# Score bursts of up to six PSUM banks, and whole projection tiles between them, in a four-layer spectral and attention kernel

## The chip, the cores and the metric

The kernel runs on one core of one Trainium2 chip. The metric is the device time of one execution in microseconds (us). Each time shown is of a whole execution of the program on the device.

## What is computed

The input `x` has 2048 rows of 512. Four layers follow one another, each a residual on a layer norm: spectral mixing (A), segmented attention with a memory (B), A again and B again. All arithmetic is on 32-bit values.

```python
    def _A_ref(x, dft_seq_re, dft_seq_im, dft_hid_re, dft_hid_im):
        a = jnp.einsum("bsd,ed->bse", x, dft_hid_re)
        b = jnp.einsum("bsd,ed->bse", x, dft_hid_im)
        y = jnp.einsum("ts,bse->bte", dft_seq_re, a) - jnp.einsum("ts,bse->bte", dft_seq_im, b)
        return y
...
        for s in range(N):
            qs, ks, vs = q[:, :, s], k[:, :, s], v[:, :, s]
            logits = jnp.einsum("bhqd,bhkd->bhqk", qs, ks) * scale + mask
            p = _softmax(logits, axis=-1)
            a_dot = jnp.einsum("bhqk,bhkd->bhqd", p, vs)
            pq = phi(qs)
            num = jnp.einsum("bhld,bhde->bhle", pq, M)
            den = jnp.einsum("bhld,bhd->bhl", pq, z)[..., None] + 1e-6
            a_mem = num / den
            o = g * a_mem + (1.0 - g) * a_dot
            outs.append(o)
            pk = phi(ks)
            M = M + jnp.einsum("bhld,bhle->bhde", pk, vs)
            z = z + jnp.einsum("bhld->bhd", pk)
        o = (lambda x, *d: x.transpose(*d))(jnp.stack(outs, 2).reshape(B, H, S, Dh), 0, 2, 1, 3).reshape(B, S, D)
        return o @ wo

    x = A_x
    x = x + _A_ref(_layernorm(x, axis=-1), A_dft_seq_re, A_dft_seq_im, A_dft_hid_re, A_dft_hid_im)
    x = x + _B_ref(_layernorm(x, axis=-1), B_wq, B_wk, B_wv, B_wo, B_beta)
```

In B there are 32 heads of 16 columns, and 4 segments of 512 rows. Within a segment the softmax attention is causal; what earlier segments left is read through the memory `M` and `z`.

## The kernel before, in words

**Units, groups, segments.** An attention layer works segment by segment. A segment's 32 heads are four groups of eight heads, and a group is two units of four heads. A unit's four heads lie as two pairs: two ranges of partitions (`SIDES`, from rows 0 and 64) hold two heads each, so that one head of each side is multiplied at the same time on half of TensorE's rows each. There are 32 units in a layer and two attention layers.

**What is done for a unit.** `stack` (line 788) loads the queries and keys of the four heads from DRAM into the two row ranges. `natural_max` (line 811) computes the scores with queries on the partitions, in five steps; each step writes two PSUM banks, which VectorE reads with `tensor_tensor_reduce` (line 835) to take each row's maximum. The steps are, for each of the two heads of a side, query tile 3 alone and then tiles 0 and 2 together, and at last tile 1 of both heads. A sixth step turns the maxima into a high and a low part (`mparts`, lines 852 and 853). `max_rows` (line 859) transposes them on TensorE, copies them out on ScalarE (line 868) and writes them by DMA as two more rows beneath the stacked queries (line 871). `softmax_values` (line 877) then computes the scores transposed, with keys on the partitions and the maximum already subtracted, again in five steps of two banks. ScalarE takes a ReLU of the diagonal blocks (line 903) and the exponential of the bank (line 904); GpSimd zeroes what lies above the diagonal (`causal`, line 907). A last step, `pv`, multiplies the probabilities with the values: 16 products of 32 output columns, which fill one bank (`pv_bank`), copied out by ScalarE (line 969). `output` (line 978) transposes that back, scales it and adds it into `o_nat`.

**The other TensorE work.** `proj` (line 732) makes the queries or the keys of a group in one bank from twelve matmuls (four slices of the 512 columns, three products each, since a 32-bit value is split into a high and a low part). `values` (line 711) and `outproj` (line 1090) do the same for a tile of 128 rows. Besides these there are transposes (`prep`, `transpose_out`) and the memory's reads and updates (`mem_read`, `mem_update`). All these use the full array of 128 rows; the scores use 50 or 48 rows of each half, the `pv` products 32 columns each.

**PSUM.** Every TensorE result goes to a tile of one tag, `bank` (line 114), with eight buffers. A tile is free again when its last reader is done.

**The order of the work** is written out by hand. Every function above is a generator; `place` (line 186) puts its next step into a numbered slot with an order number inside the slot, and at the end all slots are run in order (lines 1287 to 1290). TensorE's instructions keep exactly this order (`keep_in_program_order`); the order on the other engines comes from the scheduler at build time, with a raised priority for the maxima (`URGENT`).

A unit has ten slots (`SU`), a group 20 (`SG`), a segment 80 (`SS`). Unit n starts at `t = t0 + 10 n`. Its softmax steps are in slots t, t+2, t+4, t+6 and t+8, its `pv` in t+12. The natural steps are in t-18 to t-10, two slots apart, so that softmax steps of one unit and natural steps of the next but one fall into the same even slots: five bursts of four banks in each unit, ten in a group. `max_rows` is in t-5 and `stack` in t-22. Projections, values and output tiles put three matmuls into a slot, over four slots (line 1215 and the lines above it). `light` (line 1162) names the slots of a unit that may take them, and `among` (line 1165) spreads eight steps over a stretch.

Of the kernel before, what the change touches and what calls it, by code (L numbers as in the profile page):

```python
# [10 lines left out]
F32 = mybir.dt.float32  # L11
# [7 lines left out]
P = 128  # L19
S, D, H = 2048, 512, 32  # L20
DH = D // H
NSEG = 4
# [36 lines left out]
def spectral_infini_kernel(  # L59
# [621 lines left out]
    def place_attention(x_in, x_out, t0, w_at, out_at):  # L681
# [195 lines left out]
        def softmax_values(s, g, u):  # L877
            qs, ks = stacks.pop((s, g, u, "q")), stacks.pop((s, g, u, "k"))
            K = KROWS + MROWS
            h0 = g * HG + u * HU  # L880

            def scores(dst, *cols):
                banks = [bank("sT") for _ in SIDES]
                off, diag = 0, []
                for p, kt in cols:
                    n = 512 - kt * P
                    for a, at in enumerate(SIDES):
                        T.matmul(
                            banks[a][:, off : off + n],
                            ks[at : at + K, p, kt * P : (kt + 1) * P],  # L890
                            qs[at : at + K, p, kt * P :],
                            start=True,
                            stop=True,
                        )
                    diag.append(off // P)
                    off += n
                for a, ps in enumerate(banks):
                    blocks = ps.rearrange("p (b c) -> p b c", c=P)
                    blocks = blocks[:, diag[0] : diag[-1] + 1 : max(1, diag[-1] - diag[0])]
                    if x_out is out_tiles and (s * NG + g) * NU + u >= NSEG * USEG - 3 and a:  # L900
                        V.tensor_scalar_max(blocks, blocks, 0.0)
                    else:
                        A.activation(blocks, blocks, AF.Relu)  # L903
                    A.activation(dst[a], ps, AF.Exp, scale=-SCALE)  # L904

            def causal(blocks):
                G.affine_select(  # L907
                    blocks,
                    blocks,
                    pattern=[[0, n] for n in blocks.shape[1:-1]] + [[1, P]],  # L910
                    compare_op=ALU.is_ge,
                    fill=0.0,
                    base=0,
                    channel_multiplier=-1,
                )
# [12 lines left out]

            p0, p1 = [], []
            events = {}  # L930

            def ev(t, f):
                events.setdefault(t, []).append(f)

            for p in range(HP):

                def first(p=p):
                    t = pair("pT", "wd", 8, F32)
                    p0.append(t)
                    scores((t[:, 0], t[:, 1]), (p, 0))  # L940
                    causal(t[:, :, :P])

                def second(p=p):
                    t = pair("pT", "wd", 8, F32)
                    p1.append(t)
                    scores((t[:, 0], t[:, 1]), (p, 1), (p, 3))
                    for c in 0, 3 * P:
                        causal(t[:, :, c : c + P])

                ev(6 + 2 * p, first)  # L950
                ev(2 + 2 * p, second)
            p2 = []

            def third():
                t = sb.tile([P, HU, 256], F32, name="pT2", tag="craw", bufs=2)
                p2.append(t.rearrange("p (a b) s -> p a b s", b=HP))
                scores([t[:, a * HP : (a + 1) * HP].rearrange("p h s -> p (h s)") for a in range(2)], (0, 2), (1, 2))
                causal(t[:, :, :P])

            ev(0, third)  # L960

            def last():
                pb = bank("pv_bank")
                pv(pb, 0, p0, 0)
                pv(pb, 1, p1, 0)
                pv(pb, 3, p1, 384)
                pv(pb, 2, [p2[0][:, :, p] for p in range(HP)], 0)
                ot = sb.tile([P, 512], F32, name="ot", tag="ut", bufs=8)
                A.activation(ot, pb, AF.Copy)
                outs[s, g, u] = ot  # L970

            ev(12, last)
            for t in range(13):
                for f in events.get(t, ()):
                    f()
                yield

        def output(s, g, u):
            ot = outs.pop((s, g, u))
# [179 lines left out]
        def unit(n):  # L1159
            return n // USEG, n % USEG // NU, n % NU  # L1160

        def light(t, n=SU):
            return [k for k in range(t, t + n) if (k - t0) % SU not in (2, 4)]

        def among(start, stop, n):
            at = light(start, stop - start)
            return [at[k * len(at) // n] for k in range(n)]

        def post(t):
            return [t + 1, t + 2, t + 3]  # L1170

# [2 lines left out]
            src = rows((wq, wk, wv, wo)[k // DT], d)  # L1174
            place(3, load_split(ws, (n, d), src, f"w{n}", "w", 16), [w_at(k) - 3, w_at(k)])
        for n in range(NSEG * USEG):
            t = t0 + SU * n
            place(0, softmax_values(*unit(n)), run_from(t, 13))
            place(1.9, output(*unit(n)), [t + 14])
            place(1.9, max_rows(*unit(n)), [t - (6 if x_out is out_tiles and n == NSEG * USEG - 1 else 5)])  # L1180
            place(1, natural_max(*unit(n)), run_from(t - 18, 5, 2), [t - 9])
            place(0.5, stack(*unit(n)), [t - 22])
        for s in range(NSEG):
            b = t0 + SS * s
            for j in range(2):
# [19 lines left out]
            for g in range(NG):  # L1205
# [126 lines left out]
```

## Time and profile before

| | |
|---|---|
| median of 3 runs | 1788.8 us (1785.93 to 1789.73) |
| the profiled execution | 1787.75 us, of which its span 1786.0 us |
| TensorE busy | 1745.4 us (98%), 10192 matmuls |
| VectorE busy | 1383.1 us (77%) |
| ScalarE busy | 1071.3 us (60%) |
| GpSimd busy | 357.7 us (20%) |
| mean granted TensorE clock | 0.993 |

The span is what the profiler records from the first instruction to the last; the execution's own time is a little longer. Names in the profile: `sT` is a bank of `softmax_values`, `nat` one of `natural_max`, `pT` the probabilities, `pqk` a projection, `pvv` a value tile, `po` an output tile, `on` and `oT` transposes of the outputs, `mT` the transpose of the maxima, `pM`, `pm` and `pkT` the memory's work, `m`, `u` and `y` the spectral layer. All matmuls have line 84, since a helper records them. PE is TensorE's matmuls, DVE VectorE, ACT ScalarE, POOL GpSimd, SPq the queue of the engine that issues most DMAs. A row of the timeline gives the start, the time to the end of the last one merged in it, and the count. Matmuls overlap in the records, so what TensorE spends on a row is read from its start to the start of the next.

### The profile page before, as it was taken

What the parts mean: (1) busy time and instruction counts of PE and PEld (TensorE: products, weight loads), DVE (VectorE), ACT (ScalarE), POOL (GpSimd) and SP (SyncE); (2) the same over time, 40 slices, a digit from 0 to 9 for tenths busy, and PEclk for the clock granted to TensorE, in tenths of its full rate; (3) what the DMA queues carried; (4) which work ended last, traced back from release to release, by engine and by line L of the source; (5) the groups of instructions that cost most, each with busy time, mean ns of one, the idle gap of its engine ahead of it and who ended that gap; (6) DMA issues with size and microseconds to landing.
All of it is one profiled execution on the core that took longest, in us unless ns stands there. A gap on an engine that the chain in (4) does not pass through costs nothing. (4 is left out here: it accounts for less than half of the span.)

```text
span 1786.0 us, 32579 instructions
## 1 busy us (share of the span) xinstructions
PE 1745.4 (98%) x10192; PEld 1266.5 (71%) x10192; DVE 1383.1 (77%) x4114; ACT 1071.3 (60%) x2388; POOL 357.7 (20%) x673
## 2 busy tenths in 40 slices
PE   8999999999999999999999999999999999999998
PEld 6888777887656666666578888888875666666655
DVE  8888978864777888877977997667658778787775
ACT  3344443432688777777764665444328787877775
POOL 1000000002232334344410000000123333333332
PEclk9999999999999999999999999999999999999999
DMA  8787775355455454555666877645546555555351
GB/s 284 244 263 254 232 249 167 106 177 159 143 153 139 142 147 111 157 129 130 170 207 215 264 236 232 195 147 149 176 130 183 134 131 151 132 132 155 91 131 44
DMA packets 145499, 303.10 MB, mean 170 GB/s; under 512 B 18096, under 2 KB 22192, under 8 KB 145328
## 3 DMA queue, kind: packets, MB, share of 16 engines
q1 hardware_dynamic: 138416, 288.44, 54.7%
q10 hardware_dynamic: 6912, 12.59, 1.8%
q8 instruction: 82, 1.34, 0.3%
q14 instruction: 89, 0.73, 0.1%
HBM read 211.83 MB, written 88.08 MB: 168 GB/s over the span
## 5 line engine op out<-in xcount | busy, mean ns | idle before, releaser
L835 DVE CUSTOM_DVE_ANT_0 junk<-nat,mask 128x512 bf16<-128x512 f32 (+3 forms) x1024 | 497.2, 486 | 178.9 <-PE nat L84 133.4
L904 ACT ACTIVATE pT<-sT 128x512 f32<-128x512 f32 x640 | 351.3, 612 | 0.7
L84 PE MATMUL m<-chi,xa 128*128 128x512 f32 x1056 | 308.6, 392 | 2.5 <-DVE c L524 2.1
L907 POOL TENSOR_SCALAR_AFFINE_SELECT pT<-pT 128x256 f32<-128x256 f32 (+1 forms) x448 | 193.3, 445 | 566.5 <-ACT pT L904 434.0
L84 PE MATMUL m<-clo,xa 128*128 128x512 f32 x720 | 230.8, 392 | 5.5 <-DVE clo L100 5.5
L84 PEld LDWEIGHTS m<-chi,xa 128*128 128x128 f32 x1056 | 198.1, 189 | 46.6 <-DVE c L524 2.9
L903 ACT ACTIVATE sT<-sT 128x256 f32<-128x256 f32 x625 | 179.7, 331 | 64.4 <-PE sT L84 63.5
L84 PE MATMUL y<-wdt,us 128*128 128x512 f32 x768 | 182.5, 391 | 0.2 <-DVE wdt L100 0.2
L84 PE MATMUL nat<-stkk,stkq 48*128 48x512 f32 (+3 forms) x1024 | 159.2, 345 | 8.4 <-DMA stkk<-scrk 5.6
L84 PE MATMUL sT<-stkq,stkk 50*128 50x256 f32 (+3 forms) x1024 | 164.8, 373 | 1.0 <-DMA stkq<-mt 0.8
L84 PEld LDWEIGHTS y<-wdt,us 128*128 128x128 f32 x768 | 143.4, 188 | 30.7 <-DVE wdt L100 0.9
L84 PEld LDWEIGHTS sT<-stkq,stkk 50*128 50x128 f32 x1024 | 84.4, 186 | 113.4 <-issue 53.0
L84 PEld LDWEIGHTS m<-clo,xa 128*128 128x128 f32 x720 | 135.2, 188 | 37.8 <-DVE clo L100 10.0
L84 PE MATMUL pv_bank<-pT,v_all 128*32 128x512 f32 (+3 forms) x2048 | 152.2, 437 | 1.7 <-DVE mx L835 1.7
L98 ACT ACTIVATE chi<-cring 128x512 fp32r<-128x512 f32 (+1 forms) x138 | 99.6, 727 | 86.0 <-PE m L84 35.8
L84 PEld LDWEIGHTS pv_bank<-pT,v_all 128*32 128x32 f32 x2048 | 59.2, 110 | 84.1 <-issue 82.8
L84 PE MATMUL pqk<-xT,wq 128*128 128x512 f32 x384 | 116.9, 425 | 0.0
L84 PEld LDWEIGHTS nat<-stkk,stkq 48*128 48x128 f32 x1024 | 96.5, 189 | 27.2 <-ACT pT L904 7.7
L84 PE MATMUL po<-wo,oh 128*128 128x512 f32 x384 | 114.5, 419 | 0.7 <-ACT oh L98 0.5
L147 POOL TENSOR_TENSOR r<-ve,half_neg 128x2 f32<-128x2 f32 (+2 forms) x24 | 19.9, 830 | 472.9 <-DVE ve L145 469.5
L84 PE MATMUL pvv<-wv,xT 128*128 128x512 f32 x384 | 114.1, 417 | 0.0
L84 PE MATMUL pqk<-xT,wk 128*128 128x512 f32 x384 | 108.5, 410 | 2.0 <-DVE mx L835 2.0
(187 smaller groups left out, 2830.4 us busy)
## 6 DMA issues: line engine op xcount, KB each, us to landing
cring<-in_ct SPq DMA_DIRECT2D x97, 256.0 KB
scrk<-parts SPq DMA_DIRECT2D x96, 256.0 KB
stkq<-scrq SPq DMA_DIRECT2D x128, 192.0 KB
stkk<-scrk SPq DMA_DIRECT2D x128, 192.0 KB
cring<-sum SPq DMA_DIRECT2D x95, 256.0 KB
xt<-mid SPq DMA_DIRECT2D x64, 256.0 KB
scrq<-parts SPq DMA_DIRECT2D x32, 512.0 KB
cring<-in_ct SPq DMA_DIRECT2D x27, 512.0 KB
```

Source lines behind the costliest of these rows:

```text
L84: return tc.keep_in_program_order(op(*args, **kwargs))
L98: pin(A.activation(hi, src, AF.Copy, scale=scale))
L147: G.tensor_tensor(out=r, in0=ve, in1=half_neg[:, :n], op=ALU.pow)
L835: last_max[0] = V.tensor_tensor_reduce(junk[:, :n], src, mask[:, 512 - n :], 1.0, 3e38, ALU.add, ALU.min, dst,)
L903: A.activation(blocks, blocks, AF.Relu)
L904: A.activation(dst[a], ps, AF.Exp, scale=-SCALE)
L907: G.affine_select(blocks, blocks, pattern=[[0, n] for n in blocks.shape[1:-1]] + [[1, P]], compare_op=ALU.is_ge, fill=0.0, base=0, channel ...
```

## The change

Two things are placed differently; no computation changes. Slots below are counted from `c`, the start of a group.

- **Scores.** The two units of a group get lists of their own. The first has its softmax steps in slots 0, 0, 3, 6 and 6 and its `pv` just before slot 12; the second in 9, 12, 12, 15 and 15 and just before slot 20. The natural steps, for the group that follows, are in 3, 3, 6, 9 and 9 (first unit) and 12, 15, 18, 18 and 20 (second unit). So the score steps fall into the slots 0, 3, 6, 9, 12, 15 and 18: seven bursts, six of three steps (six banks) and the last of two. The softmax steps take the order that they had: tile 2 of both heads, tiles 1 and 3 of each head, tile 0 of each head.
- **Tiles of twelve.** A projection, value or output tile puts its twelve matmuls into one slot: queries in slot 13 and keys in slot 16 for most groups, values at slots 4 and 7, output tiles at slots 1 and 7. The first two projections of a layer stay as they were, as do the output tiles of the last segment.

`max_rows` moves to 6 slots before the first unit's first softmax step (5 for the second), and `stack` to 7 slots before the first natural step (5 for the second unit).

```diff
-            p0, p1 = [], []
-            events = {}
...
-                ev(6 + 2 * p, first)
-                ev(2 + 2 * p, second)
...
+            def step(*cols):
+                t = pair("pT", "wd", 8, F32)
+                scores((t[:, 0], t[:, 1]), *cols)
+                for c in range(0, 512, 384)[: len(cols)]:
+                    causal(t[:, :, c : c + P])
+                return t
+
+            t = sb.tile([P, HU, 256], F32, name="pT2", tag="craw", bufs=2)
+            scores([t[:, a * HP : (a + 1) * HP].rearrange("p h s -> p (h s)") for a in range(2)], (0, 2), (1, 2))
+            causal(t[:, :, :P])
+            p2 = t.rearrange("p (a b) s -> p a b s", b=HP)
+            yield
+            p1, p0 = [], []
             for p in range(HP):
...
+                p1.append(step((p, 1), (p, 3)))
                 yield
+            for p in range(HP):
+                p0.append(step((p, 0)))
+                yield
+            pb = bank("pv_bank")
...
-            t = t0 + SU * n
-            place(0, softmax_values(*unit(n)), run_from(t, 13))
-            place(1.9, output(*unit(n)), [t + 14])
-            place(1.9, max_rows(*unit(n)), [t - (6 if x_out is out_tiles and n == NSEG * USEG - 1 else 5)])
-            place(1, natural_max(*unit(n)), run_from(t - 18, 5, 2), [t - 9])
-            place(0.5, stack(*unit(n)), [t - 22])
+            c = t0 + SG * (n // NU)
+            if n % NU == 0:
+                at, nat, pv_at, load, turn = (0, 0, 3, 6, 6), (3, 3, 6, 9, 9, 10), 12, -24, -6
+            else:
+                at, nat, pv_at, load, turn = (9, 12, 12, 15, 15), (12, 15, 18, 18, 20, 21), 20, -13, 4
+            if n == 0:
+                load = -22
+            place(0, softmax_values(*unit(n)), [c + k for k in at], [c + pv_at - 0.1])
+            place(1.9, output(*unit(n)), [c + pv_at + 2])
+            place(1.9, max_rows(*unit(n)), [c + turn])
+            place(1, natural_max(*unit(n)), [c - SG + k for k in nat])
+            place(0.5, stack(*unit(n)), [c + load])
...
-            place(2, values(s), *([light(b - 20), light(b)] if s else [run_from(b - 18, 8), light(b - 10)]))
+            place(2, values(s), *([k] * DT for k in ((b - 36, b - 16, b + 4, b + 7) if s else (b - 17, b - 13, b - 7, b - 2))))
...
-                free = light(o + 20) + light(o + 40) if s < NSEG - 2 else run_from(o + 20, DT * LT, 3)
+                free = [o + k for k in ((21, 27, 41, 47) if s < NSEG - 2 else (21, 27, 47, 67)) for _ in range(DT)]
...
-                    (0, 2): among(b, b + 13, 8),
-                    (0, 3): among(b + 13, b + 29, 8),
-                    (1, 0): among(b - 40, b - 29, 8),
-                    (1, 1): among(b - 29, b - 17, 8),
-                }.get((s, g), light(t - 50))
+                    (0, 2): [b + 1] * 4 + [b + 10] * 4,
+                    (1, 0): [b - 38] * 4 + [b - 33] * 4,
+                }.get((s, g), [t - 47] * 4 + [t - 44] * 4)
```

More of the change, by code (lines that the diff above doesn't have):

```diff
@@ L927, in pv @@
                     )
-            p0, p1 = [], []
-            events = {}
-            def ev(t, f):
-                events.setdefault(t, []).append(f)
-            for p in range(HP):
[L937 to L948, printed above, removed]
-                ev(6 + 2 * p, first)
-                ev(2 + 2 * p, second)
@@ L952, in softmax_values @@
[L952 to L975, printed above, removed]
-                yield
+            def step(*cols):
[6 more added lines that the diff above has]
+            scores([t[:, a * HP : (a + 1) * HP].rearrange("p h s -> p (h s)") for a in range(2)], (0, 2), (1, 2))
@@ new lines, in softmax_values @@
+            causal(t[:, :, :P])
+            p2 = t.rearrange("p (a b) s -> p a b s", b=HP)
+            yield
+            p1, p0 = [], []
+            for p in range(HP):
+                p1.append(step((p, 1), (p, 3)))
+                yield
+            for p in range(HP):
+                p0.append(step((p, 0)))
+                yield
+            pb = bank("pv_bank")
+            pv(pb, 0, p0, 0)
+            pv(pb, 1, p1, 0)
+            pv(pb, 3, p1, 384)
+            pv(pb, 2, [p2[:, :, p] for p in range(HP)], 0)
@@ L978, in output @@
+            ot = sb.tile([P, 512], F32, name="ot", tag="ut", bufs=8)
+            A.activation(ot, pb, AF.Copy)
+            outs[s, g, u] = ot
+            yield
         def output(s, g, u):
@@ L1160, in unit @@
             return n // USEG, n % USEG // NU, n % NU
[L1162 to L1167, printed above, removed]
         def post(t):
```

## The prediction

> **What bounds the kernel now.** I read the page first, for the engines' shares.
>
> ```profile
> span 1786.0 us, 32579 instructions
> PE 1745.4 (98%) x10192; PEld 1266.5 (71%) x10192; DVE 1383.1 (77%) x4114; ACT 1071.3 (60%) x2388; POOL 357.7 (20%) x673
> ```
>
> TensorE is busy nearly throughout, but its ends are modelled, so the share cannot say whether it runs at its peak. The windows view compares a stretch of the spectral layer with one segment (eight units) of attention.
>
> ```profile
> 1150.00:1200.00 50.00, 50.00 (x223) 41.40 (x222) 30.87 (x48) 23.40 (x37) 0.00 (x0) 1.00 0.55 171
> 580.40:697.10 116.70, 116.60 (x857) 76.50 (x856) 95.05 (x380) 90.17 (x224) 42.27 (x81) 1.00 0.52 137
> ```
>
> The columns are PE, PEld, DVE, ACT and POOL busy time. In the spectral stretch a 512-column matmul costs 50/223 = 0.224 us; the change leaves that layer alone. In attention a group (two units) takes 116.7/4 = 29.2 us, in which VectorE is busy 23.8 us and ScalarE 22.5 us. TensorE is the bound, and the other two are close behind. What TensorE does in that time shows in the timeline, by its start times.
>
> ```profile
> 661.71 0.50 PE L84 MATMUL sT<-stkq,stkk 50*128 50x512 f32 x2
> 662.05 0.40 PE L84 MATMUL nat<-stkk,stkq 48*128 48x512 f32 x2
> 662.38 1.66 PE L84 MATMUL pvv<-wv,xT 128*128 128x512 f32 x6
> 663.97 0.50 PE L84 MATMUL sT<-stkq,stkk 50*128 50x512 f32 x2
> ...
> 668.35 1.65 PE L84 MATMUL pqk<-xT,wq 128*128 128x512 f32 x6
> 669.93 2.36 PE L84 MATMUL pv_bank<-pT,v_all 128*32 128x512 f32 x32
> ...
> 672.22 0.50 PE L84 MATMUL sT<-stkq,stkk 50*128 50x384 f32 x4
> ```
>
> From 661.71 to 663.97 is 2.26 us. The two score steps each run two matmuls side by side on half the rows (50 or 48 of 128). If such a pair costs what one full 512-column matmul does, the stretch is 8 x 0.224 = 1.79 us of streaming. The other 0.47 us is the price of leaving the full array for the half-row form and coming back, so 0.235 us a change of form. The six matmuls from 668.35 to 669.93 take 1.58 us against 1.34, again 0.24 us over. TensorE's loss in attention is thus changes of form, not idle time.
>
> Two places of the same trace show what limits longer bursts: the eight banks of PSUM.
>
> ```profile
> 842.74 0.50 PE L84 MATMUL sT<-stkq,stkk 50*128 50x384 f32 x4
> 843.08 0.44 PE L84 MATMUL nat<-stkk,stkq 48*128 48x512 f32 x1
> 844.43 0.47 PE L84 MATMUL nat<-stkk,stkq 48*128 48x512 f32 x1 [0.91 <-DVE mparts L852]
> ```
>
> ```profile
> 1723.96 0.51 PE L84 MATMUL sT<-stkq,stkk 50*128 50x512 f32 x2
> ...
> 1724.30 0.41 PE L84 MATMUL nat<-stkk,stkq 48*128 48x512 f32 x2
> ...
> 1724.53 0.42 PE L84 MATMUL sT<-stkq,stkk 50*128 50x512 f32 x2
> ...
> 1725.49 0.56 PE L84 MATMUL nat<-stkk,stkq 48*128 48x128 f32 x4 [0.55 <-ACT pT L904]
> ```
>
> At 842.74 a four-bank burst stands right behind a value stage with little else near it: its last bank is still being read by VectorE, and TensorE waits 0.91 us. At 1723.96 eight banks are asked for in a row. The last step waits until ScalarE has finished the exponentials of the first, 1.53 us after that began.
>
> **The change, part by part: fewer changes of form.** By the slot lists, a group has had ten score bursts and two value stages, each stage directly ahead of a burst: 10 entries, 10 exits, 2 extra at the value stages, 22 changes. Afterwards there are seven bursts. Five are followed by full-array work (10 changes). The bursts of slots 9 and 18 go straight into a value stage and from it into the burst of slots 12 and 20 (4 changes). That is 14, 8 fewer. I take 0.225 us for one, a little under the measured 0.235 because those around the value stage are not separately seen: 8 x 0.225 = 1.8 us a group, and 32 groups (16 in each attention layer) make **58 us** off. If a sixth of them lie under a bank wait that is there anyway, it is 48 us.
>
> **Bank waits that come in.** What six banks take to drain follows from these rows of ScalarE, VectorE and GpSimd.
>
> ```profile
> 657.96 0.65 ACT L903 ACTIVATE sT<-sT 128x256 f32<-128x256 f32 x2
> 658.52 1.09 ACT L904 ACTIVATE pT<-sT 128x512 f32<-128x512 f32 x2
> ...
> 662.31 0.44 ACT L903 ACTIVATE sT<-sT 128x128 f32<-128x128 f32 x2
> 662.68 1.09 ACT L904 ACTIVATE pT<-sT 128x512 f32<-128x512 f32 x2
> ...
> 672.36 0.60 ACT L969 ACTIVATE ot<-pv_bank 128x512 f32<-128x512 f32 x1 [2.44 <-PE pv_bank L84]
> ```
>
> ```profile
> 658.15 0.69 DVE L835 CUSTOM_DVE_ANT_0 junk<-nat,mask 128x512 bf16<-128x512 f32 x1 [0.74 <-PE nat L84]
> ...
> 659.61 0.08 DVE L835 DVE_READ_ACCUMULATOR2_ANT mx<- 128x1 f32 x1
> ...
> 668.46 0.42 DVE L835 CUSTOM_DVE_ANT_0 junk<-nat,mask 128x256 bf16<-128x256 f32 x1 [0.17 <-PE nat L84]
> ...
> 670.32 0.09 DVE L835 DVE_READ_ACCUMULATOR2_ANT mx<- 128x1 f32 x1
> ...
> 675.45 0.28 DVE L835 CUSTOM_DVE_ANT_0 junk<-nat,mask 128x128 bf16<-128x128 f32 x1
> ...
> 677.19 0.08 DVE L835 DVE_READ_ACCUMULATOR2_ANT mx<- 128x1 f32 x1
> ```
>
> ```profile
> 659.67 0.77 POOL L907 TENSOR_SCALAR_AFFINE_SELECT pT<-pT 128x256 f32<-128x256 f32 x2 [2.80 <-ACT pT L904]
> ```
>
> First to last, a softmax step of two blocks holds ScalarE 1.65 us, one of key tile 0 1.46 us. A natural step of tile 3 (A) holds VectorE 1.54 us, the mixed one (B, 675.45 to 677.27) 1.82 us, the last (C, 668.46 to 670.41) 1.95 us. TensorE writes a step in 0.34 us, a further one of the same burst in 0.23 (1724.30 to 1724.53), so a burst of six banks in about 0.9 us. By bursts:
> - Slots 12 and 20, behind a value stage. The burst of slot 9 leaves VectorE B and C, 3.8 us; that of slot 18 A and B, 3.4 us. The value stage passes 2.29 us (669.93 to 672.22) and its own bank is held 0.74 us more (to 672.96). So the next burst, 3.2 us after the last one began, finds two or three of the eight banks taken and asks for six. The like of it is the 0.91 us row; the last bank is wanted only 0.6 us into the burst, so I take 0.5 us each, **1.0 us** a group.
> - Slot 3. In half the groups no output tile stands at slot 1, so only four transposes separate the bursts of slots 0 and 3 (0.49 us, next rows). The second starts about 1.65 us after the first, when one bank is untouched and one has come back (at 1.5 us). Its last step gets its banks at about 3.1 us, against 2.2, and the maxima of C, read by the transpose in slot 4, are ready at 3.5. I take 1.3 us there, **0.65 us** over all groups.
> - The value stage of the first unit needs the softmax steps of slot 6: 0.5 + 2 x 1.46 + 0.4 us of GpSimd, 3.8 us after the burst. TensorE gets there later where a tile of twelve stands between (12 x 0.224 = 2.7 us), about 0.9 us earlier where none does: **0.3 us** over all.
> - The bursts of slots 6, 9, 15 and 18 overlap the former one's drain by little: 0.1 us each, **0.4 us**.
>
> ```profile
> 675.07 0.66 PE L84 MATMUL on<-ident,ot 128*128 128x128 f32 x4
> 675.56 0.27 PE L84 MATMUL mT<-ident,mparts 128*72 128x128 f32 x1
> ```
>
> That is 2.35 us a group. Some of it replaces waits of today (the 0.91 us row is one); I credit 0.15 us. 32 x 2.2 = **70 us** on.
>
> **Edits that I cost at nothing.** The twelve matmuls in one go hold their bank 2.7 us in place of four or five slots; this is what lets six banks go to a burst, and it is in the sum. Stack loads and maxima rows move relative to their users:
>
> ```profile
> L868 ACT ACTIVATE mt<-mT 32x128 fp32r<-32x128 f32 x64 | 16.5, 258 | 7.2 <-PE mT L84 7.2
> ```
>
> ```profile
> 1738.15 5.37 DMA stkk<-scrk
> ...
> 1757.36 0.62 SPq L871
> ...
> 1758.03 1.92 DMA stkq<-mt
> ```
>
> A slot is 29.2/20 = 1.46 us. A load has had 4 slots (5.8 us) to its first use and gets 7 and 5 (10 and 7 us), so 5.4 us stays covered, the SP queue's own issues included. It must still wait for the buffer's last reader, now one slot ahead of it. The maxima have had 5 slots to the softmax and get 6 and 5, for 0.3 + 0.6 + 1.9 us. Uncovered, either costs about 1 us a group; a lead gained is worth nothing, since neither is waited for in most groups now. The last group of layer two has the same score work and no projections either way: 0, give or take 3 us.
>
> The sum is against the profiled execution's 1787.75 us (1786.0 of span and 1.75 around it; the median of the runs shown is 1.05 above): 1787.75 - 58 + 70 = **1800 us**.
>
> [...]
>
> **The rivals.**
> - *The changes of form decide* (faster). ScalarE and VectorE have 5 to 7 us free in each group of 29.2. If drains start earlier than I reckon, only the bursts behind the value stage wait, 0.9 us a group: 1787.75 - 58 + 29 = 1759 us; with no new wait at all, 1730. For it: at 1723.96 even eight banks in a row cost only 0.55 us. Against it: that burst found nothing else in PSUM.
> - *They cancel*: net waits of 1.7 to 1.9 us a group, 1785 to 1791 us.
> - *The maxima come late* (slower still). The row transpose of the second unit, slot 4, needs C of slot 0, and behind it hang the maxima's DMA and the softmax of slot 9. Where slots 1 to 3 are empty and VectorE is behind by over 1 us, this adds 1 us a group, 32 us: 1832 us.
> - *The clock falls.* Windows with waits have shown less than full clock:
>
> ```profile
> 500.00:550.00 50.00, 48.24 (x329) 30.75 (x328) 37.50 (x155) 41.36 (x104) 16.36 (x31) 0.93 0.52 140
> ```
>
> Here 7% of 50 us is lost, 3.5 us. If half the groups lost as much, it would be 56 us: 1856 us. Against it: steady segments with short waits run at 1.00. [...]
> - *The change does not do what it says*: TensorE's order is pinned, so the slot lists are what runs; no chance of its own.
>
> **How the numbers follow.** My forecast, waits above savings, 0.46; changes of form decide, 0.35; cancel, 0.09; late maxima, 0.07; clock, 0.03. So slower 0.56, same 0.09 (0.2% is 3.6 us, about what a measurement of this kernel can tell from no change), faster 0.35. The forecast's own part goes from 1792 to 1830 (waits of 3.1 us a group with no credit: 99 us on, 58 off). The rival on the fast side enters the range down to its 1759; what it has below, about 0.1, and the slow ones above 1832, about 0.08, stay out.
>
> **What would show it.** Right: in TensorE's timeline 14 changes of form a group, twelve projection matmuls in about 2.9 us, and waits of 0.3 to 1.3 us inside bursts released by ACT pT or DVE mx, most behind the value stage and at slot 3; VectorE's and ScalarE's busy totals as before. Wrong: steady groups under 28.5 us with bursts of six written in under 1.2 us; or the long waits standing at the row transpose or at a DMA; or a change of form that costs well under 0.2 us.

## The result, and the profile after

The changed kernel takes 1866.38 us (median of 4 runs, 1864.14 to 1872.38), the kernel before 1787.37 us in the runs beside it (1781.36 to 1789.73). The ratio is 1.045, with a 95% interval from 1.0415 to 1.049: slower by 79 us. The forecast was 1800 us, slower, with a range from 1759 to 1832 us.

The page of the changed kernel's profiled execution (1864.14 us), from the top:

```profile
span 1862.3 us, 32611 instructions
PE 1783.6 (96%) x10192; PEld 1334.9 (72%) x10192; DVE 1397.6 (75%) x4114; ACT 1067.3 (57%) x2388; POOL 358.4 (19%) x673
...
PEclk9999999999799999999899999999998999999998
```

VectorE, ScalarE and GpSimd do what they did before, to about 1%. The row of the granted clock was nothing but nines before; now it has a seven and three eights. The mean granted clock fell from 0.993 to 0.966. The traces record it as 1.00 or 0.50 and as nothing between (23 stretches at 0.50 in this span, 6 before), so twice what is missing to 1 is the share of time at half clock: 2 x 0.034 x 1862.3 = 127 us, against 25 us before.

The windows of the changed kernel show the spectral stretch, and the segment that the prediction took its 116.70 us from:

```profile
1150.00:1200.00 50.00, 50.00 (x222) 41.42 (x221) 30.85 (x48) 23.40 (x37) 0.00 (x0) 1.00 0.63 195
596.10:721.90 125.80, 120.87 (x858) 85.75 (x856) 96.45 (x382) 89.99 (x225) 42.27 (x81) 0.96 0.46 127
```

The spectral stretch is as it was. The segment, eight units with the same work, takes 9.1 us more, 2.3 us a group; at a clock of 0.96, 4% of 125.8 us or 5.0 us of that is clock.

TensorE's timeline of the changed kernel, in a stretch of that segment in which nothing goes wrong, and then where it does:

```profile
596.13 2.36 PE L84 MATMUL pv_bank<-pT,v_all 128*32 128x512 f32 x32
598.42 0.79 PE L84 MATMUL sT<-stkq,stkk 50*128 50x384 f32 x8
599.05 0.69 PE L84 MATMUL nat<-stkk,stkq 48*128 48x512 f32 x2
599.67 0.73 PE L84 MATMUL pm<-state,phi 128*128 128x136 f32 x4
600.29 3.02 PE L84 MATMUL pqk<-xT,wq 128*128 128x512 f32 x12
603.15 0.60 PE L84 MATMUL on<-ident,ot 128*128 128x128 f32 x4
```

```profile
581.12 0.74 PE L84 MATMUL sT<-stkq,stkk 50*128 50x256 f32 x8
581.70 0.46 PE L84 MATMUL nat<-stkk,stkq 48*128 48x256 f32 x4
582.09 0.66 PE L84 MATMUL on<-ident,ot 128*128 128x128 f32 x4
582.98 0.74 PE L84 MATMUL sT<-stkq,stkk 50*128 50x384 f32 x4 [0.24 <-DVE mx L835]
584.02 0.80 PE L84 MATMUL nat<-stkk,stkq 48*128 48x512 f32 x3 [0.30 <-DVE mx L835]
585.10 0.55 PE L84 MATMUL nat<-stkk,stkq 48*128 48x128 f32 x3 [0.27 <-DVE mx L835]
586.36 0.27 PE L84 MATMUL mT<-ident,mparts 128*72 128x128 f32 x1 [0.72 <-DVE mparts L853]
586.39 4.57 PE L84 MATMUL pvv<-wv,xT 128*128 128x512 f32 x12
590.89 0.73 PE L84 MATMUL sT<-stkq,stkk 50*128 50x512 f32 x4
591.46 0.40 PE L84 MATMUL nat<-stkk,stkq 48*128 48x512 f32 x2
591.79 2.99 PE L84 MATMUL pvv<-wv,xT 128*128 128x512 f32 x12
```

At 598.42, right behind a value stage, a burst of six banks takes 1.25 us without a bracket, and at 600.29 twelve matmuls take 2.86 us: the plan works as meant. At 581.12 a group begins in which no tile stands between slots 0 and 3. The burst of slot 3 comes 1.86 us after the first one; its banks come back one by one, and the row transpose of slot 4 waits for the maxima: 0.24 + 0.30 + 0.27 + 0.72 = 1.53 us in brackets. Then the next twelve matmuls take 4.50 us, although nothing releases them late. The windows of that place show why:

```profile
583.00:586.00 3.00, 2.07 (x10) 1.30 (x10) 2.90 (x14) 3.00 (x9) 1.40 (x3) 1.00 0.38 143
587.00:590.40 3.40, 3.40 (x10) 2.62 (x9) 1.73 (x8) 0.00 (x0) 0.36 (x1) 0.51 0.04 10
590.40:594.00 3.60, 3.60 (x19) 2.48 (x18) 1.40 (x4) 3.00 (x9) 0.41 (x1) 0.99 0.41 96
```

While it waits, TensorE still has the full clock. In the 3.4 us right after, the granted clock is 0.51, and then it is full again. Waits of 1.53 us in all were followed by some 1.7 us more, half of the 3.4 us, that no bracket shows.

**Where the 76 us of span went.** I split TensorE's time, from each matmul's start to the next one's, into four parts: streaming at full clock (with what lies ahead of the first matmul, 1579 us in all runs), changes of form (counted in TensorE's order; undisturbed ones cost 0.20 us on average), what matmuls in half-clock stretches took longer, and the rest. The rest is waits, and pairs that ran one after the other because one bank came late. All but the count is worked out from start times.

| kernel | time, us | changes of form | their cost | lost to the clock | waits |
|---|---|---|---|---|---|
| before | 1787.4 | 720 | 146 | 11 | 50 |
| after | 1866.4 | 464 | 93 | 58 | 132 |
| after less before | +79 | -256 | -53 | +47 | +82 |

The three differences make +76, the difference of the spans (1862.3 - 1786.0). The clock's part and the waits are estimates. Of the 126 us that the changed kernel's trace has at half clock TensorE stood idle for some 12, and half of the rest, 57 us, is the most that can be lost there. A second count from the same records, with slightly other streaming times, gives +43 for the clock and +85 for the waits, so the two are good to about 5 us.

### The profile page after: what moved, and what is told of

It reads as the page before. It is cut to its first block, busy times and chain, and to the rows that moved or that the text cites. A ratio compares the mean times of both kernels' runs of the same rounds, so it can differ in the third digit from the quotient of the medians.

```text
span 1862.3 us, 32611 instructions
## 1 busy us (share of the span) xinstructions
PE 1783.6 (96%) x10192; PEld 1334.9 (72%) x10192; DVE 1397.6 (75%) x4114; ACT 1067.3 (57%) x2388; POOL 358.4 (19%) x673
## 4 chain that ended last, share of the span: by engine, by line
PE 65%; DVE 15%; ACT 4%; issue 3%; DMA 1%; POOL 0%; DVEq 0%; ACTq 0%; POOLq 0%
PE m L84 19%; PE pqk L84 9%; PE pv_bank L84 7%; PE y L84 7%; DVE junk L835 6%; PE pvv L84 5%; PE po L84 5%; PE nat L84 4%; PE sT L84 4%; ACT pT L904 1%; DVE c L524 1%; PE pm L84 1%; PE pM L84 1%; ACT sT L903 1%; PE on L84 1%
## 5 line engine op out<-in xcount | busy, mean ns | idle before, releaser
L84 PE MATMUL nat<-stkk,stkq 48*128 48x512 f32 (+3 forms) x1024 | 171.5, 360 | 10.2 <-DVE otmp L984 2.7
L84 PE MATMUL pv_bank<-pT,v_all 128*32 128x128 f32 (+3 forms) x2048 | 169.4, 458 | 0.3
L84 PE MATMUL sT<-stkq,stkk 50*128 50x256 f32 (+3 forms) x1024 | 146.1, 360 | 6.5 <-DVE mx L835 2.9
L84 PEld LDWEIGHTS nat<-stkk,stkq 48*128 48x128 f32 x1024 | 104.1, 192 | 51.6 <-ACT pT L904 14.0
L84 PEld LDWEIGHTS pv_bank<-pT,v_all 128*32 128x32 f32 x2048 | 71.3, 114 | 79.3 <-issue 63.1
L84 PE MATMUL pvv<-wv,xT 128*128 128x512 f32 x384 | 108.9, 438 | 1.6 <-DVE mx L835 1.6
L84 PE MATMUL po<-wo,oh 128*128 128x512 f32 x384 | 105.6, 425 | 1.2 <-ACT oh L98 0.5
L766 POOL TENSOR_TENSOR parts<-praw,parts 128x512 fp32r<-128x512 f32 x64 | 82.2, 1285 | 113.4 <-ACT parts L765 100.0
L84 PE MATMUL pqk<-xT,wk 128*128 128x512 f32 x384 | 101.9, 411 | 1.6 <-DVE otmp L984 1.6
```

Source lines behind the costliest of these rows:

```text
L84: return tc.keep_in_program_order(op(*args, **kwargs))
L766: G.tensor_tensor(out=parts[:, 1], in0=raw, in1=parts[:, 0].bitcast(F32), op=ALU.subtract)
```

## The experiments

The theory (W): the six-bank bursts bring waits for banks, the waits bring the clock down, and the two together outweigh the changes of form that are saved. The rivals differ a little from run to run. D is that thin work, the scores and transposes that use part of the array or few columns, brings the clock down, waits or not. Q is that the loss comes from queues standing behind a late weight load in each layer's first segment, and for the input transposes that they wait for something other than the maxima. The runs of which a ratio is given are timed in three rounds; the others are single runs, beside one run of the kernel before at 1785.5 us. The four runs of the changed kernel lie within 8 us, so a single run settles no smaller difference.

**1. The bursts alone.** The changed kernel, with the matmuls of projection, value and output tiles spread as before.

```diff
-            place(2, values(s), *([k] * DT for k in ((b - 36, b - 16, b + 4, b + 7) if s else (b - 17, b - 13, b - 7, b - 2))))
+            place(2, values(s), *([light(b - 20), light(b)] if s else [run_from(b - 18, 8), light(b - 10)]))
```

(and likewise for output tiles and projections)

> The changed kernel with the score bursts of the change alone: projections, values and output tiles go back to three matmuls a slot, in the slots that they had. Theory W (bank waits): the changed kernel loses where two bursts follow one another with no tile between, TensorE waits there for VectorE and ScalarE to free banks, and these waits of some 3 us in a row also bring the clock to half (127 us at half clock against 27 before). Spread tiles put some full matmuls behind every burst, so the waits and most of the half-clock time go and the saved changes of form stay: 1740 to 1790 us, half clock under 60 us. Rival D (thin work): half-row and transpose work counts little for the clock, waits or not; the stretches between are now fuller, so about the same as W. Rival Q (engine queues in order): the loss comes from VectorE and SP queues that stand behind a late weight load in each layer's first segment: 1845 us or more, as the loads are unmoved.

It took 1817.3 us, with 532 changes (107 us), 18 us of clock and 112 us of waits. Its mean clock:

```profile
core 0: 1815.6 us, clock 0.990
```

The half clock is down as theory W had it (2 x 0.010 x 1815.6 = 36 us of it), but the time misses W's band, because the waits stay. Rival Q, at 1845 us or more, is out. Against before this is -39 for form, +62 for waits and +7 for the clock: the six-bank bursts by themselves make the kernel 30 us slower. The other 49 us of the change come with the twelve matmuls in one go, and some 40 of those are clock.

**2. The tiles alone.** The kernel before, its values, output tiles and projections in the slots of the changed one.

> The kernel before with the other half of the change alone: bursts of four banks in every second slot as before, but twelve matmuls of a tile in one slot, at the slots of the change. Theory W: most pairs of bursts then have nothing between them, run together into eight banks and wait: 1830 to 1900 us, half clock over 100 us. Rival D: the same stretches are thin, so half clock over 100 us too, but little waiting in the score steps: 1800 to 1830 us. Rival Q: 1790 to 1800 us.

It took 1960.2 us, past every band. Of the 512-column natural steps the view of instruction groups, shapes kept apart, says:

```profile
L84 PE MATMUL nat<-stkk,stkq 48*128 48x512 f32 x256 | 92.3, 463 | 57.2 <-DMA stkk<-scrk 37.7 <-ACT pT L904 14.8 <-ACT sT L903 1.5
```

TensorE is idle 57.2 us ahead of these matmuls (the group's number behind the last bar, with its releasers), and 37.7 of them are waits for the load of the stacked keys, which the changed kernel issues seven or five slots ahead of its use and this one four. Its mean clock is 0.963, which is 145 us at half clock; W and D both had over 100. The run therefore prices another mismatch too, and does not tell what whole tiles cost with bursts of four.

**3. A quicker drain.** TensorE's order is that of the changed kernel, but VectorE reads 64 columns of each natural block in place of 128 to 512. This leaves out most of the row maximum; the exponent is scaled down so that it stays finite.

```diff
-                    n = src.shape[1]
+                    n = 64
...
-                            junk[:, :n], src, mask[:, 512 - n :], 1.0, 3e38,
+                            junk[:, :n], src[:, :n], mask[:, :n], 1.0, 3e38,
...
-                    A.activation(dst[a], ps, AF.Exp, scale=-SCALE)
+                    A.activation(dst[a], ps, AF.Exp, scale=-SCALE / 1000)
```

> The changed kernel, with VectorE reading only 64 columns of each natural score block for the maximum, and a thousandth of the exponent's scale so that all values stay finite: it leaves out most of the row maximum, so that natural banks come free in about half the time or less. TensorE's order, its number of changes of form and its work are those of the changed kernel. Theory W: the waits on natural banks and on the maxima's transpose, some 45 of the 66 us that came in, go, and half clock falls to under 50 us: 1730 to 1775 us. Rival D: half clock stays over 90 us of the 127, since the work is as thin as before: 1790 to 1815 us. Rival Q: the late weight split of the first segment stays, 1835 us or more.

It took 1784.3 us. Its page, and its mean clock:

```profile
PE 1731.4 (97%) x10192; PEld 1303.9 (73%) x10192; DVE 1150.3 (65%) x4114; ACT 1061.8 (60%) x2388; POOL 358.6 (20%) x673
```

```profile
core 0: 1782.5 us, clock 0.989
```

VectorE is busy 247 us less, and TensorE, with the same matmuls in the same order, works at 0.989 in place of 0.966: 18 us lost to the clock against 58, and waits of 92 us against 132. Half clock is 2 x 0.011 x 1782.5 = 39 us, under W's 50 and far from D's 90: the same thin work in the same order does not bring the clock down by itself, and with some 40 us of waits 40 us of the clock's loss go. The time lies 9 us above W's band: 42 us of waits over those of before are left, which the quicker drain does not take away.

**4. Waits in the order of before.** The kernel before, with the transpose of the maxima rows four slots earlier, right behind the maxima.

```diff
-            place(1.9, max_rows(*unit(n)), [t - (6 if x_out is out_tiles and n == NSEG * USEG - 1 else 5)])
+            place(1.9, max_rows(*unit(n)), [t - 9])
```

> The kernel before with the transpose of the maxima right behind the last natural step, four slots earlier, so that TensorE stops at it until VectorE has finished the maxima: one wait of 1.5 to 2.5 us for each of 64 units. The work around it is as dense as before and the changes of form are 724 against 720. Theory W (waits bring the clock down): besides 100 to 150 us of waiting, half clock rises from 27 to over 100 us: 1920 to 2000 us. Rival D (only thin work brings it down): half clock stays under 40 us: 1885 to 1930 us.

It took 2012.3 us. In turn the row of the transposes in the view of instruction groups, the mean clock, and one unit of the timeline:

```profile
L84 PE MATMUL mT<-ident,mparts 128*72 128x128 f32 x64 | 21.9, 342 | 159.1 <-DVE mparts L853 140.3 <-ACT pT L904 14.4 <-ACT parts L765 4.5
```

```profile
core 0: 2010.5 us, clock 0.945
```

```profile
658.97 0.97 PE L84 MATMUL po<-wo,oh 128*128 128x512 f32 x3
662.75 0.43 PE L84 MATMUL mT<-ident,mparts 128*72 128x128 f32 x1 [2.81 <-DVE mparts L853]
662.83 1.63 PE L84 MATMUL po<-wo,oh 128*128 128x512 f32 x3
664.26 1.05 PE L84 MATMUL oT<-ident,onat 128*128 128x128 f32 x4
```

One wait in each of 64 units, 2.5 us on average, puts TensorE at half clock for 2 x 0.055 x 2010.5 = 221 us. Three matmuls behind the wait take 1.43 us (662.83 to 664.26), against 3 x 0.224 = 0.67. Bursts and tiles are those of before, where 25 us were at half clock, so here it is the added waits that bring the clock down; D had under 40 us. The time is 12 us over W's band.

**5. Single waits of the changed kernel.** Two waits stood out in the same view of the changed kernel beside that of the kernel before. Rows of the changed kernel:

```profile
L84 PE MATMUL xnT<-ident,xn 128*128 128x128 f32 x128 | 21.2, 291 | 11.5 <-DVE xn L168 11.4
...
L84 PE MATMUL mT<-ident,mparts 128*72 128x128 f32 x64 | 18.9, 295 | 22.8 <-DVE mparts L853 17.4 <-DVE mx L835 2.2 <-DVE den L1005 1.3
```

and of the kernel before:

```profile
L84 PE MATMUL xnT<-ident,xn 128*128 128x128 f32 x128 | 20.2, 281 | 6.1 <-DVE xn L168 6.1
...
L84 PE MATMUL mT<-ident,mparts 128*72 128x128 f32 x64 | 17.9, 279 | 0.4 <-DVE mparts L853 0.4
```

The maxima's transpose was waited for by 0.4 us in all, and now by 22.8. That is slot 4, and the first edit puts it into slot 5:

```diff
-                at, nat, pv_at, load, turn = (9, 12, 12, 15, 15), (12, 15, 18, 18, 20, 21), 20, -13, 4
+                at, nat, pv_at, load, turn = (9, 12, 12, 15, 15), (12, 15, 18, 18, 20, 21), 20, -13, 5
```

> The changed kernel with the transpose of the second unit's maxima one slot later (slot 5 in place of 4), behind the value tile that stands in slot 4 of three groups in four. Theory W: the waits of 0.7 to 1.2 us ahead of that transpose, some 16 us over the kernel, go where a value tile covers them, and the half-clock windows that begin right behind them (at 587, 682, 709, 808 and 836 us in the first layer) go with them: half clock from 127 to 100 us or less, 1835 to 1852 us. Rival D (thin work, waits or not): the waits go, half clock stays at 120 us or more: 1850 to 1858 us.

1854.8 us: waits 12 us down (the transpose's idle time is 9.5 us), the half clock not (61 us lost, against 58).

```profile
core 0: 1853.1 us, clock 0.964
```

That is 133 us at half clock, so the time and the clock of this single run are those of rival D, and W missed: taking this one wait away does not bring the clock back.

For the input transposes `xnT`, the changed kernel's windows have a granted clock of 0.57 around the longest of the waits, and its timeline shows that one:

```profile
492.00:512.00 20.00, 13.70 (x69) 8.38 (x73) 14.73 (x55) 11.44 (x28) 3.78 (x8) 0.57 0.51 120
```

```profile
501.32 1.11 PE L84 MATMUL xnT<-ident,xn 128*128 128x128 f32 x4
507.89 1.09 PE L84 MATMUL xnT<-ident,xn 128*128 128x128 f32 x4 [5.46 <-DVE xn L168]
508.90 3.85 PE L84 MATMUL pv_bank<-pT,v_all 128*32 128x512 f32 x32
```

My first theory was that loads and splits of the output weights hold VectorE up. Two runs move these loads, six slots ahead and forty back:

```diff
-            place(3, load_split(ws, (n, d), src, f"w{n}", "w", 16), [w_at(k) - 3, w_at(k)])
+            place(3, load_split(ws, (n, d), src, f"w{n}", "w", 16), [w_at(k) - (3 if k < 3 * DT else 9), w_at(k)])
```

```diff
-        return lambda k: b - 52 + 2 * k if k < 12 else b + 20 + 5 * (k - 12)
+        return lambda k: b - 52 + 2 * k if k < 12 else b + 60 + 5 * (k - 12)
```

> The changed kernel, with the four loads of the output weights nine slots ahead of their split in place of three. Theory W: the wait of 5.8 and 4.6 us at the input transposes in each layer's first segment goes (there VectorE's queue stands behind the split of a weight that lands 6 us after its issue), and the 17 and 14 us at half clock around it: 15 to 25 us off, 1840 to 1852 us. Rival Q: far more of the loss hangs on this queue: under 1820 us. If the waits there come from something else: 1862 to 1868 us.

> The changed kernel with the four loads and splits of the output weights 40 slots later, out of each attention layer's first segment. With these loads nine slots earlier, the wait of 4.5 us at the input transposes stayed, as the load was still issued late. If that wait hangs on the weights at all (VectorE stands behind the split of one that has not landed): the waits of 5.8 and 4.6 us and most of 31 us of half clock near them go, 25 us off, 1835 to 1848 us. If the transposes wait for something else (the row loads or the maxima that VectorE does first): above 1856 us.

1856.3 and 1875.2 us, with the wait in its place in both (9.7 and 9.8 us of idle time). The first time lies between the outcomes that were expected, the second in that of other causes. That theory fell. The next one: the second tile is normalised on VectorE behind the maxima of slot 9's burst (`behind_max`, line 697), and TensorE transposes it two slots later with nothing between. The test puts the transpose three slots later:

```diff
-                place(2, prep(s, (2 * j, 2 * j + 1)), [*(t - d for d in first), t, t, t + 2])
+                place(2, prep(s, (2 * j, 2 * j + 1)), [*(t - d for d in first), t, t, t + (5 if s == 1 else 2)])
```

> The changed kernel, with the transposes of the second of two input tiles (xnT, second segment) three slots later. Theory P: they wait because VectorE normalises that tile behind the maxima of slot 9's burst; with three slots between, xnT's start-to-start time on TensorE falls from 26.9 us to under 19, the half clock around 495 to 512 us (17 us of it) goes, and the time is 1845 to 1858 us. Rival Q: they wait for something that does not move with VectorE's maxima (the load of the rows, a buffer), so xnT keeps over 24 us and the time is 1860 to 1872 us. Second rival D: the wait goes, and the half clock turns up elsewhere (over 120 us of it in all), 1858 to 1868 us.

1852.4 us; the ratio to before is 1.038 (1.036 to 1.040), and the row now reads

```profile
L84 PE MATMUL xnT<-ident,xn 128*128 128x128 f32 x128 | 21.3, 295 | 1.4 <-DVE xn L168 1.4
```

Theory P holds for the wait and the time. The half clock near 500 us shrank from 17 to 10 us, but did not go.

> As the run before, and the maxima rows of the second unit one slot later (turn 5 for 4). If the clock's loss is the sum of single waits, each worth what it is worth alone, the two edits add: 1835 to 1848 us. If the dips are set by the general density of waits in a group, and a wait removed only moves them, the time is 1850 to 1862 us with over 115 us at half clock.

Both edits together: 1838.9 us, ratio 1.031 (1.028 to 1.034). The steps from 1.045 over 1.038 to 1.031 are equal, so the edits add up. In the split, waits are down 13 us and the clock's loss 14 us from those of the changed kernel (18 and 10 us in the second count): a microsecond of wait saved brought 0.6 to 1.1 us of clock.

**6. What a change of form costs.** The kernel before, with each slot's tile matmuls between its softmax and its natural step: the full array twice in each burst.

```diff
-            place(2, values(s), *([light(b - 20), light(b)] if s else [run_from(b - 18, 8), light(b - 10)]))
+            place(0.7, values(s), *([light(b - 20), light(b)] if s else [run_from(b - 18, 8), light(b - 10)]))
```

(and likewise for output tiles and projections)

> The kernel before with the matmuls of projections, values and output tiles placed between the softmax step and the natural step of the same slot instead of behind both. It has 1014 changes of form against 720, the same work and as many banks asked for in a row or fewer. If a change costs the 0.21 us that the changed kernel's timeline shows, 294 more of them make 62 us: 1835 to 1855 us, with half clock as before (27 us). If the loss at a change is mostly something that other waiting hides, under 1815 us.

1832.9 us with 1014 changes, 294 more. In its timeline

```profile
608.66 0.50 PE L84 MATMUL sT<-stkq,stkk 50*128 50x512 f32 x2
609.09 0.96 PE L84 MATMUL po<-wo,oh 128*128 128x512 f32 x3
609.98 0.50 PE L84 MATMUL nat<-stkk,stkq 48*128 48x512 f32 x2
610.41 0.97 PE L84 MATMUL po<-wo,oh 128*128 128x512 f32 x3
```

three tile matmuls take 0.89 us (609.09 to 609.98) against 3 x 0.224 = 0.67, and the burst's halves are 0.43 us each against 0.34. The time is 47 us more, 0.16 us a change; the split has 62 us of form, 0.21 us a change, and 17 us of waits less, presumably since each burst now asks for two banks at a time. The prediction's 0.225 us a change is a little high against both; its trade of changes against waits stands.

**7. Putting it together.** The spread tiles of the first run with both edits of the fifth group, and then the same with the natural steps in slots of their own, so that fewer bursts ask for six banks:

```diff
-                at, nat, pv_at, load, turn = (0, 0, 3, 6, 6), (3, 3, 6, 9, 9, 10), 12, -24, -6
+                at, nat, pv_at, load, turn = (0, 0, 3, 6, 6), (2, 4, 6, 8, 9, 10), 12, -24, -6
...
-                at, nat, pv_at, load, turn = (9, 12, 12, 15, 15), (12, 15, 18, 18, 20, 21), 20, -13, 5
+                at, nat, pv_at, load, turn = (9, 12, 12, 15, 15), (13, 15, 17, 18, 20, 21), 20, -13, 5
```

> The seven bursts with the tiles' matmuls spread as before, and with the two later steps (second segment's transposes three slots later, the second unit's maxima rows one slot later). If the two edits save waits wherever they stand, they are worth 15 to 28 us again: 1789 to 1803 us. If spreading had already hidden those waits, it stays at 1808 to 1820 us. In neither case is it expected to beat the kernel before.

> As the run before, and the natural steps apart from the softmax steps (slots 2, 4, 6, 8, 9 and 13, 15, 17, 18, 20), so that fewer bursts ask for six banks; TensorE changes form 810 times in place of 530. If a change costs 0.16 to 0.21 us, this adds 45 to 59 us; if the waits left (some 90 us) come from the six-bank bursts, 30 to 60 us of them go. Sum: 1785 to 1825 us, with nat's start-to-start time on TensorE back under 160 us. If the waits do not come from the size of the bursts, they stay and it is 1835 to 1860 us.

1811.5 us (ratio 1.015, 1.013 to 1.017) and 1824.7 us (1.022, 1.020 to 1.024). The first lies in the band of its second case, in which spreading had already hidden the waits: beside spread tiles the two edits are worth 6 us, not 15 to 28, though that is set against the first experiment's single run. That case's reason does not quite hold, since the idle time at `xnT` was 13.2 us in the first experiment and is 2.0 here: the wait went, and less time with it. The second is inside its time band, but the natural steps did not come back under 160 us of TensorE's time (165). From the one to the other there are 280 changes of form more (106 to 165 us) and 43 us of waits fewer (104 to 61), with the clock's loss at 19 and 22 us. The sum, +19, is the difference of the spans. So between these two the larger bursts are worth having: 59 us of form against 43 us of waits, at nearly the same clock. But the order of the kernel before, with bursts of four, has fewer changes than the second and fewer waits than either, and no version that computes the whole was faster than it.

## Why the prediction was wrong

**What bounds the kernel** held: TensorE, with its changes of form and its eight banks.

**Changes of form: right.** 14 a group as predicted; 720 to 464 is 8 fewer in each of 32 groups. They saved 53 us where 58 were forecast (0.20 us each and not 0.225).

**Bank waits: nearly right in sum, 82 us where 70 were forecast, but not in place.** The forecast put its largest part, 1.0 us a group, into the bursts right behind a value stage. Taken from start to start and less their streaming, these 62 bursts cost 0.54 us each before and 0.55 us after, so waits there only replaced those of before. The waits came to the bursts with no tile since the last burst: 13 such bursts cost 15 us before, 46 cost 70 us after. Sixteen of these stand in slot 3, with 2.2 us each, what follows the burst included; a burst that waits for nothing costs 0.27 us. So slot 3's 1.3 us was too low, and the bursts of slots 6, 9, 15 and 18, priced at 0.1 us each, took 0.5 to 1.0 us over that where no tile stands ahead. Part of the missing 12 us stands at input transposes that the diff does not touch: the prediction listed the steps that move, and this one stands still while the burst ahead of it grew. Their idle time went from 6.1 to 11.5 us.

**Edits costed at nothing: right but for one.** The loads of the stacks stay covered. The transpose of the maxima rows in slot 4 is a slot too early; the forecast had it inside the price of slot 3, the rival of late maxima had it at 32 us, and the row has 22.8 us of idle time, more than any other group of TensorE's. Long waits at this transpose were one of the prediction's own signs of being wrong. One slot later it is 9.5.

**The clock: the step that failed.** The prediction had a fall of the clock as a rival that excludes the forecast, at a chance of 0.03 and at 56 us, and argued against it that "steady segments with short waits run at 1.00". Its size was nearly right (47 us). But it is no other case: the waits that the forecast itself added brought the clock down where little other work stood around them. The fourth experiment shows waits doing so without the change (159 us of them at one transpose, a clock of 0.945), the third that the loss goes with VectorE's part of them (132 to 92 us of waits, 58 to 18 lost to the clock), and the first that it also goes, with most of the waits left, when the tiles' matmuls are spread among the bursts (112 us of waits, 18 lost). Had the term stood in the sum, 1787.75 - 58 + 70 + 56 gives 1856 us. The evidence against it came from segments with 50 us of waits over the whole run; it could say nothing about a kernel that was to have 120. Nor need a single wait be long: the window at 587.00 has 0.51 behind waits of at most 0.72 us each.

**What the clock follows, and what stays open.** The clock's loss does not follow the sum of the waits alone. Bursts with spread tiles have 104 to 112 us of waits and lose 18 or 19 us; the changed kernel has 132 and loses 58, and with the rows one slot later it has 120 and loses 61. The 14 traces say more. The recorded changes of the granted clock lie multiples of 3.413 us apart, to within 3 ns (all 11 in the trace of the kernel before, all 47 in that of the changed one). I cut each trace on such times into stretches of that length, took those at full clock and added up what TensorE streamed in each, by start-to-start times of the same traces: 0.227 us for a full 512-column matmul or a pair of score matmuls, 0.43 us for four `pv` products, fewer columns in proportion, 0.109 us for a 128-column transpose. Of 6749 stretches with at least half of their time streamed, none was followed by half clock; of 136 with under 0.35, 131 were; between them it was 114 of 256. The stretch ahead of 587.00 has 0.32. Stretches under 0.43 number 6 in the kernel before, 25 in the changed one, 7 with spread tiles, 11 with the quick drain and 44 in the fourth experiment. So in these runs half clock went with how little was streamed in the stretch ahead of it. Waits were the main way there and not the only one: of all 245 falls, 33 follow a stretch with under a tenth of idle time. What decides between 0.35 and 0.5 stays open.

## What to carry to other kernels

Where TensorE waits often and little full-array work stands between the waits, price a wait at up to about twice its length: here 1.53 us of waits were followed by 3.4 us at half clock, some 1.7 us lost, in which nothing looked late, because the engine's rows were simply longer. Full-array matmuls spread among the bursts kept that price away here (112 us of waits, 18 us lost to the clock); the same matmuls in one piece did not (132 and 58 us). So a term of waits and a term of clock belong in the same sum, not in two rivals. And when a burst is made larger, look at every step that depends on the engine that drains it, also at those that the change leaves where they were.

## What the runs showed of the hardware

- The granted clock was recorded as 1.00 or 0.50, and the half-clock stretches that end within the spans of the kernel before and the changed one lasted 3.41 us or a multiple, up to 17.07. Waits of 1.53 us in sum within some 3.6 us were enough for one (those up to 586.36 in the changed kernel, with 0.51 from 587.00). But waits of 1.46 and 2.51 us in the fourth experiment (ahead of 626.48 and 645.99) had none behind them: from 600 to 650 its clock was 1.00. A stretch of 3.41 us with at least half of it streamed was never followed by half clock (6749 of them), one with under 0.35 nearly always (131 of 136).
- A change between the full array and the half-row form of the scores cost 0.16 to 0.21 us, by the 294 added ones of the sixth experiment.
- The two matmuls of a score step can start together: in the 512-column natural steps the second started under 0.03 us behind the first in 90 of 128 pairs before, and in 70 of 121 after that stand next to each other in the trace. When one came late, as at 843.08 and 844.43 in the kernel before, they ran one after the other: the second started over 0.2 us behind the first in 18 of the 128 before, and in 41 of the 121 after. Start to start, the natural steps took 150 us of TensorE's time before and 184 us after. Some 12 us of that is idle time in brackets, mostly of the maxima's transpose behind them, and part of the rest is half clock.
